# Attention's loads and stores wait, besides their product, for the landing that leaves at most 1.2 MB under way

## The chip, the cores and the metric

The kernel runs on one core of a Trainium2 chip. The metric is device microseconds (us) of one execution. Engines are named as the profile names them: PE (TensorE, matrix products), PEld (its weight loads), DVE (VectorE), ACT (ScalarE), POOL (GpSimd), SP (SyncE, which here only issues transfers).

## The reference

Attention over 8 batches, 8 heads, 576 positions and 64 dimensions, followed by a mixture of experts. In heads 0 to 3 a position sees the 32 positions up to itself, in heads 4 to 7 every fourth of the 128 positions up to itself:

```python
scores = scale * np.matmul(q, k.transpose(0, 1, 3, 2))
mask_plain = (rel >= 0) & (rel < window)                              # window 32
mask_dil = (rel >= 0) & (rel < window * dilation) & (rel % dilation == 0)   # dilation 4
scores = np.where(masks[None, :, :, :], scores, -1000000000.0)
attn = np.exp(scores - np.max(scores, axis=-1, keepdims=True))
attn = attn / (np.sum(attn, axis=-1, keepdims=True) + 1e-09)
out = np.matmul(attn, v)
```

The result, 4608 tokens of 512 numbers, goes through 8 experts. Each takes the 576 best tokens by `logits = x @ w_gate` (all pairs sorted, each token placed once) and computes `np.maximum(x @ w1[e], 0.0) @ w2[e]`.

## The kernel before

**Stages.** In the first 190 us or so the kernel computes attention and writes its rows into a scratch tensor `xd` in HBM, and prepares the choice of tokens. Behind it come eight rounds of expert products, which gather their tokens from `xd` and fetch weights. The change touches attention alone.

**Attention.** There are 32 units: per batch two kinds of heads (kind 0 plain, kind 1 dilated, in the names p and d) and two pairs of heads of each. For a batch and a kind SP issues two loads of q (`qs`, L376), two of k (L378) and two of v (L288). `qs` is then spread into `q` with zeros between (L389 on DVE and POOL, L284 on ACT; of kind 0 three of the four copies are POOL's, and the first pair of heads takes both of its halves from POOL). v is shifted into two other groups of partitions (L295, L297), from the second batch on by POOL alone. Per unit PE makes scores in bf16 for the row maxima (L492, L496), DVE reduces them, PE makes the scores in float32 (L503, L508), ACT takes the exponential (L462), PE multiplies with v (L515, L520), DVE divides (L528 to L530) into `xs`, and PE transposes the result (L579) for the gate's logits. Once a kind of a batch is done, SP stores `xs` into `xd` (L539): two transfers for kind 0, eight small ones for kind 1. q, k and v have two buffers for each kind, used in turn by the batches.

**What sets the order.** Attention is planned when the program is built: `Schedule.run` places every operation on its engine by estimated costs and due times, and each engine works its list off in order. SP's list is thus fixed: an instruction that waits holds up all loads and stores behind it. What a load or store of attention waits for is written by `paced` (L315). `K.gate` is the last product of a unit's scores, values or transposes that the plan has ended 0.2 us after the transfer's planned time at the latest; `after` makes the transfer wait for it. `LIMIT` is 1200e3 bytes and `flow` the list of earlier transfers. As long as the plan has no such product, the transfer waits for the landing of the earlier transfer with which it and all between them would be over 1.2 MB. In the kernel before this holds for the first ten loads (issued up to 7.6 us); every later one takes the `return` and waits for its product, and isn't entered into `flow`.

Besides this, each SP transfer uses one of eight completion semaphores in turn, and waits for the landing of the transfer eight places before it. The waits for buffers (q, k, v copied or used up, `xs` written) come on top.

Of the kernel before, what the change touches and what calls it, by code (L numbers as in the profile page):

```python
# [256 lines left out]
def attention(tc, ctx, C, load_const, T, xd, Lt, R):  # L257
# [5 lines left out]
    K = Schedule({"DVE": TOL_A, "ACT": TOL_B, "POOL": TOL_C, "PE": TOL_D}, True)  # L263
# [48 lines left out]
    def after(i, name, why):  # L312
        tc.add_manual_dep(i, name, mybir.DependencyInfo(mybir.DependencyClass.Sync, mybir.DependencyReason.DATA), reason=why)

    def paced(fn, bytes_):  # L315

        def run():
            i, under_way = fn().ins, bytes_
            if K.gate:
                return after(i, K.gate, "transfers keep step with the products")  # L320
            for prev, z in reversed(flow):
                under_way += z
                if under_way > LIMIT:
                    after(i, prev.name, "few bytes under way")
                    break
            flow.append((i, bytes_))

        return run
# [1182 lines left out]
```

## Time and profile before

| | us |
|---|---|
| median of 3 runs (684.36 to 690.0) | 687.72 |
| the profiled execution | 686.38 |
| its span, first to last instruction | 684.4 |

In the profile an instruction's row gives its start and length from the span's start, and in brackets the idle time of its engine before it and what ended that; "issue" means that the engine waited for nothing that the profile shows. A stretch A:B is given in us from the span's start. The landing of a transfer is when its last part is in place.

### The profile page before, as it was taken

What the parts mean: (1) busy time and instruction counts of PE and PEld (TensorE: products, weight loads), DVE (VectorE), ACT (ScalarE), POOL (GpSimd) and SP (SyncE); (2) the same over time, 40 slices, a digit from 0 to 9 for tenths busy, and PEclk for the clock granted to TensorE, in tenths of its full rate; (3) what the DMA queues carried; (4) which work ended last, traced back from release to release, by engine and by line L of the source; (5) the groups of instructions that cost most, each with busy time, mean ns of one, the idle gap of its engine ahead of it and who ended that gap; (6) DMA issues with size and microseconds to landing.
All of it is one profiled execution on the core that took longest, in us unless ns stands there. A gap on an engine that the chain in (4) does not pass through costs nothing.

```text
span 684.4 us, 18985 instructions
## 1 busy us (share of the span) xinstructions
PE 629.4 (92%) x7497; PEld 548.7 (80%) x7497; DVE 472.3 (69%) x1553; ACT 294.4 (43%) x643; POOL 207.8 (30%) x315
## 2 busy tenths in 40 slices
PE   7889887888955999999999999999999999999994
PEld 5778777677643998898799789889879989988983
DVE  6577856876668896689799689778969936714200
ACT  4646453455402835845345145234423625424210
POOL 5465576472003217433203112210320321311011
PEclk9999999999956999999999999999999999999998
DMA  8998988882203948977236115314512654203001
GB/s 245 267 273 241 211 250 243 229 225 67 73 1 116 246 78 211 259 163 235 83 95 229 47 55 184 133 55 139 177 47 66 228 201 146 69 32 102 1 26 44
DMA packets 51673, 99.09 MB, mean 145 GB/s; under 512 B 7168, under 2 KB 17152, under 8 KB 51584
## 3 DMA queue, kind: packets, MB, share of 16 engines
q1 hardware_dynamic: 42240, 72.71, 35.9%
q0 software_dynamic: 9344, 25.17, 13.6%
q8 instruction: 59, 0.97, 0.6%
q14 instruction: 30, 0.25, 0.1%
HBM read 72.69 MB, written 18.87 MB: 134 GB/s over the span
## 4 chain that ended last, share of the span: by engine, by line
PE 61%; issue 14%; DVE 14%; DMA 4%; POOL 3%; ACT 2%; SPq 0%; POOLq 0%; DVEq 0%; ACTq 0%
PE py L1378 18%; PE ph L1335 18%; PE px L520 4%; PE pS L508 4%; PE px L579 3%; PE ptx L1298 2%; PE pz L808 2%; PE py L1381 2%; PE py L1383 2%; DMA raw<-in_moe_w 1%; POOL out L1404 1%; DVE xs L530 1%; DVE hb L1356 1%; DVE mx L443 1%; DVE G L822 1%
## 5 line engine op out<-in xcount | busy, mean ns | idle before, releaser
L1378 PE MATMUL py<-w2h,hb 128*128 128x512 f32 x512 | 170.6, 399 | 0.0
L1335 PE MATMUL ph<-xh,w1h 128*128 128x256 f32 (+1 forms) x512 | 138.2, 300 | 0.0
L1335 PE MATMUL ph<-xl,w1h 128*128 128x256 f32 (+1 forms) x512 | 136.6, 297 | 0.0
L1335 PE MATMUL ph<-xh,w1l 128*128 128x256 f32 (+1 forms) x512 | 136.0, 296 | 0.0
L1378 PEld LDWEIGHTS py<-w2h,hb 128*128 128x128 f32 x512 | 96.1, 188 | 19.3
L1167 ACT ACTIVATE hb<-ph 128x256 fp32r<-128x256 f32 (+2 forms) x192 | 59.7, 345 | 95.3 <-PE ph L1335 93.9
L1404 POOL DMA_INDIRECT out<-y,idx x40 | 40.8, 1019 | 197.1 <-ACT y L1167 133.1
L1378 PE MATMUL py<-w2l,hb 128*128 128x512 f32 x256 | 99.8, 390 | 0.0
L1335 PEld LDWEIGHTS ph<-xh,w1h 128*128 128x128 f32 x512 | 91.8, 190 | 0.5
L1335 PEld LDWEIGHTS ph<-xh,w1l 128*128 128x128 f32 x512 | 91.7, 190 | 0.1
L1335 PEld LDWEIGHTS ph<-xl,w1h 128*128 128x128 f32 x512 | 91.4, 190 | 0.0
L1356 DVE SCALAR_TENSOR_TENSOR hb<-ph,hb 128x320 fp32r<-128x320 f32 (+1 forms) x128 | 56.6, 452 | 28.0 <-ACT hb L1167 25.1
L462 ACT ACTIVATE E<-pS 128x384 f32<-128x384 f32 x96 | 46.1, 489 | 56.9 <-PE pS L508 51.9
L1167 ACT ACTIVATE y<-py 128x512 f32<-128x512 f32 (+1 forms) x40 | 23.8, 596 | 92.4 <-PE py L1378 80.7
L508 PE MATMUL pS<-q,k 128*64 128x64 f32 x1152 | 54.8, 232 | 5.0 <-issue 5.0
L1284 POOL DMA_INDIRECT xg<-xd,idx x40 | 42.0, 1049 | 45.9 <-PE ph L1335 25.2
L520 PE MATMUL px<-v,E 128*64 128x65 f32 x1152 | 48.9, 226 | 6.7 <-issue 4.5
L1378 PEld LDWEIGHTS py<-w2l,hb 128*128 128x128 f32 x256 | 48.2, 188 | 8.5
L1167 ACT ACTIVATE w1h<-raw 128x512 fp32r<-128x512 f32 x64 | 40.1, 629 | 28.8 <-DMA raw<-in_moe_w 28.6
L520 PEld LDWEIGHTS px<-v,E 128*64 128x64 f32 x1152 | 43.3, 140 | 10.5 <-issue 6.7
L508 PEld LDWEIGHTS pS<-q,k 128*64 128x64 f32 x1152 | 46.0, 142 | 3.2 <-issue 3.2
L295 POOL COPY v<-v 32x520 f32<-32x520 f32 (+2 forms) x56 | 33.2, 618 | 50.2 <-DMA v<-in_vd 15.5
(193 smaller groups left out, 1110.0 us busy)
## 6 DMA issues: line engine op xcount, KB each, us to landing
raw<-in_moe_w SPq DMA_DIRECT2D x128, 256.0 KB, 3.5
qs<-in_qp SPq DMA_DIRECT2D x16, 288.0 KB, 7.0
k<-in_kp SPq DMA_DIRECT2D x16, 288.0 KB, 4.4
qs<-in_qd SPq DMA_DIRECT2D x16, 288.0 KB, 5.2
k<-in_kd SPq DMA_DIRECT2D x16, 288.0 KB, 6.8
xd<-xs SPq DMA_DIRECT2D x8, 512.0 KB, 4.9
w2l<-raw POOLq DMA_DIRECT2D x16, 256.0 KB
v<-in_vp SPq DMA_DIRECT2D x8, 325.0 KB, 7.0
```

The costliest lines, as they stand in the source:

```text
L295: f(t[:32, c0 + 1:c1 + 1], t[96:, c0:c1])
L462: e = self.op("ACT", 490, lambda j=j, pS=pS: nc.scalar.activation(self.E[:, 3 * j:3 * j + 3].rearrange("p c x -> p (c x)"), pS.tile[:, :38 ...
L508: x = nc.tensor.matmul(pS[64 * h:64 * h + 64, k, :, h], self.K[:, 32 * g:32 * g + 64], self.Q[:, g], start=False, stop=True, skip_group_ch ...
L520: x = nc.tensor.matmul(px[64 * h:64 * h + 64, c - c0, a], self.E[:, k, 64 * a:64 * a + 64], self.V[:, k, 2 * self.ui + a], start=True, sto ...
L579: x = nc.tensor.transpose(pt.tile[:, 128 * (c - c0):128 * (c - c0) + 128], xs[:, c, 2 * ui:2 * ui + 2].rearrange("p a d -> p (a d)"), C["i ...
L808: nc.tensor.matmul(o, self.ohr[:, j].rearrange("p r x -> p (r x)"), self.G[:, 4 * j:4 * j + 4, :w], start=(j == 0), stop=(j == NCH // 4 - 1))
L1167: act = lambda o, i, f=AF.Copy: nc.scalar.activation(o, i, f)
L1284: nc.gpsimd.indirect_dma_start(out=xg[:n], out_offset=None, in_=xd, in_offset=bass.IndirectOffsetOnAxis(ap=box[0][:n, m:m + 1], axis=0))
L1335: nc.tensor.matmul(o, a[:, d * 128:d * 128 + 128], b[:, d, c0:c1], start=((d, i) == pairs[0]), stop=((d, i) == pairs[-1]))
L1356: hl = op("DVE", 335 if j == 0 else 400, lambda: nc.vector.scalar_tensor_tensor(hb[:, CAP + c0:CAP + c1], o, 0.0, hb[:, c0:c1], op0=OP.max ...
L1378: nc.tensor.matmul(py, x, w, start=(f + i == 0), stop=(f == NF - 1 and i == 2))
L1404: s = nc.gpsimd.indirect_dma_start(out=out, out_offset=bass.IndirectOffsetOnAxis(ap=box[0][:n, m:m + 1], axis=0), in_=y[:n], in_offset=None)
```

## The change

One `return` goes. A transfer that waits for its product now also goes through the rule of 1.2 MB and is entered into `flow`.

```diff
         def run():
             i, under_way = fn().ins, bytes_
             if K.gate:
-                return after(i, K.gate, "transfers keep step with the products")
+                after(i, K.gate, "transfers keep step with the products")
             for prev, z in reversed(flow):
                 under_way += z
                 if under_way > LIMIT:
                     after(i, prev.name, "few bytes under way")
                     break
             flow.append((i, bytes_))
```

No instruction moves: all engines have the same rows in the same order. On SP the waits of 121 of the 450 rows differ. `DMAHW0` to `DMAHW7` are the eight completion semaphores of SP's transfers, `PE`, `DVE`, `Activation` and `Pool` those of the engines; a wait that an earlier one on SP already implies is not written. Here is SP's list in the third batch, before:

```order
L378 DMA k00_95<-in_kp 128x576 [waits DMAHW5_49,PE_49]
L288 DMA v00_103<-in_vp 64x1300 [waits DMAHW6_49,PE_49,Activation_49]
L288 DMA v00_103<-in_vp 64x1040 [waits DMAHW7_49,PE_49,Activation_49]
L539 DMA xd_66<-xs01_124 128x4x256 [waits DMAHW0_49,DVE_49,PE_49]
L539 DMA xd_66<-xs01_124 64x256 [waits DMAHW1_49,PE_49]
L376 DMA qs10_109<-in_qd 128x576 [waits DMAHW2_49,PE_49,Activation_49]
L376 DMA qs10_109<-in_qd 128x576 [waits DMAHW3_49,PE_49]
L378 DMA k10_97<-in_kd 128x576 [waits DMAHW4_49,PE_49]
```

And the same eight rows of the changed kernel:

```order
L378 DMA k00_95<-in_kp 128x576 [waits DMAHW5_49,DMAHW0_49,PE_49]
L288 DMA v00_103<-in_vp 64x1300 [waits DMAHW3_49,DMAHW6_49,PE_49,Activation_49]
L288 DMA v00_103<-in_vp 64x1040 [waits DMAHW7_49,PE_49,Activation_49]
L539 DMA xd_66<-xs01_124 128x4x256 [waits DMAHW5_49,DVE_49,PE_49]
L539 DMA xd_66<-xs01_124 64x256 [waits DMAHW1_49,PE_49]
L376 DMA qs10_109<-in_qd 128x576 [waits DMAHW2_49,DMAHW6_49,PE_49,Activation_49]
L376 DMA qs10_109<-in_qd 128x576 [waits DMAHW7_49,PE_49]
L378 DMA k10_97<-in_kd 128x576 [waits DMAHW4_49,DMAHW0_49,PE_49]
```

The store of 128x4x256 now waits for `DMAHW5`, the landing of the k load three rows above it, and the last k load for `DMAHW0`, the landing of that store, four rows above it; before, both waited for a transfer eight places back.

The second place is SP's list in the fifth batch, the last loads of kind d and the first of the next batch. Before:

```order
L378 DMA k10_97<-in_kd 128x576 [waits DMAHW6_49,PE_49]
L539 DMA xd_66<-xs01_124 128x4x256 [waits DMAHW7_49,DVE_49,PE_49]
L539 DMA xd_66<-xs01_124 64x256 [waits DMAHW0_49,PE_49]
L378 DMA k10_97<-in_kd 128x576 [waits DMAHW1_49]
L288 DMA v10_105<-in_vd 64x1300 [waits DMAHW2_49,PE_49,Pool_49]
L288 DMA v10_105<-in_vd 64x1040 [waits DMAHW3_49,PE_49,Pool_49]
L376 DMA qs01_108<-in_qp 128x576 [waits DMAHW4_49,PE_49,Pool_49]
```

And in the changed kernel:

```order
L378 DMA k10_97<-in_kd 128x576 [waits DMAHW6_49,DMAHW2_49,PE_49]
L539 DMA xd_66<-xs01_124 128x4x256 [waits DMAHW4_49,DMAHW7_49,DVE_49,PE_49]
L539 DMA xd_66<-xs01_124 64x256 [waits PE_49]
L378 DMA k10_97<-in_kd 128x576 [waits DMAHW5_49]
L288 DMA v10_105<-in_vd 64x1300 [waits DMAHW7_49,PE_49,Pool_49]
L288 DMA v10_105<-in_vd 64x1040 [waits DMAHW3_49,PE_49,Pool_49]
L376 DMA qs01_108<-in_qp 128x576 [waits DMAHW0_49,PE_49,Pool_49]
```

The first v load of kind d now waits for `DMAHW7`, the landing of the large store three rows above it, where before it waited for `DMAHW2`, a load eight places back.

## Rows read from the trace of the kernel before

**Rows 1.** Busy time by stretch: us, then busy us (and instructions) of PE, PEld, DVE, ACT, POOL, then the granted clock of PE (1.00 is 2.4 GHz), the mean busy share of the 16 DMA engines, and the GB/s that they moved.
```profile
41.00:154.70 113.70, 95.75 (x2618) 84.70 (x2616) 80.54 (x256) 57.32 (x124) 68.33 (x109) 0.98 0.89 240
3.60:11.60 8.00, 5.93 (x102) 4.83 (x101) 4.80 (x11) 3.11 (x5) 7.16 (x17) 1.00 0.97 255
...
154.70:222.00 67.30, 48.41 (x965) 36.82 (x958) 47.54 (x186) 20.69 (x47) 10.64 (x15) 0.80 0.20 60
```

**Rows 2.** PE's instructions in order of time, those in attention before which PE stood with "issue": start, length, line, operation, tiles, and in brackets the idle time.
```profile
48.51 0.46 PE L520 MATMUL px<-v,E 128*64 128x65 f32 x9 [1.12 <-issue]
70.70 0.40 PE L520 MATMUL px<-v,E 128*64 128x65 f32 x7 [1.68 <-issue]
91.66 0.51 PE L508 MATMUL pS<-q,k 128*64 128x64 f32 x11 [1.89 <-issue]
98.99 0.22 PE L503 MATMUL pS<-R,const 73*64 73x64 bf16 x3 [0.85 <-issue]
104.09 0.22 PE L508 MATMUL pS<-q,k 128*64 128x64 f32 x1 [1.00 <-issue]
109.73 0.28 PE L503 MATMUL pS<-R,const 73*64 73x64 bf16 x6 [1.97 <-issue]
115.66 0.22 PE L503 MATMUL pS<-R,const 73*64 73x64 bf16 x2 [0.79 <-issue]
120.23 0.22 PE L508 MATMUL pS<-q,k 128*64 128x64 f32 x1 [0.87 <-issue]
146.69 0.27 PE L520 MATMUL px<-v,E 128*64 128x65 f32 x1 [1.44 <-issue]
156.26 0.46 PE L508 MATMUL pS<-q,k 128*64 128x64 f32 x9 [1.21 <-issue]
```

**Rows 3.** DMA queues: packets, MB, share of 16 engines. The first row is of the whole span, the second of the stretch 89:90.2.
```profile
q8 instruction: 59, 0.97, 0.6%
...
q8 instruction: 1, 0.02, 5.3%
```

**Rows 4.** SP's transfers in order of time from 82 to 92 us: start, length, line, tiles, count.
```profile
82.12 1.86 SPq L376 DMA_DIRECT2D qs<-in_qd  x2
84.08 0.38 SPq L378 DMA_DIRECT2D k<-in_kd  x1
84.56 0.94 SPq L539 DMA_DIRECT2D xd<-xs  x2
85.56 1.11 SPq L378 DMA_DIRECT2D k<-in_kd  x1
86.77 1.26 SPq L288 DMA_DIRECT2D v<-in_vd  x2
88.26 1.90 SPq L376 DMA_DIRECT2D qs<-in_qp  x2
```

**Rows 5.** From issue to landing, of single loads, in this order, of 288 KB each: the q loads issued at 11.28, 26.93, 82.12 and 88.26 us, the k load issued at 38.54 us, and (325 KB) the v load of kind d issued at 66.38 us.
```profile
DMA to landing us min/median/max: 5.2/5.2/5.2
DMA to landing us min/median/max: 4.5/4.5/4.5
DMA to landing us min/median/max: 5.7/5.7/5.7
DMA to landing us min/median/max: 8.8/8.8/8.8
DMA to landing us min/median/max: 5.3/5.3/5.3
DMA to landing us min/median/max: 9.9/9.9/9.9
```

**Rows 6.** Issues of the whole span: tiles, operation, count, KB of one, median us from issue to landing where it is known.
```profile
qs<-in_qp SPq DMA_DIRECT2D x16, 288.0 KB, 7.0
...
xd<-xs SPq DMA_DIRECT2D x8, 512.0 KB, 4.9
...
v<-in_vp SPq DMA_DIRECT2D x8, 325.0 KB, 7.0
```

**Rows 7.** SP's transfers in order of time in the third batch, as in Rows 4.
```profile
38.54 1.47 SPq L378 DMA_DIRECT2D k<-in_kp  x2
40.12 2.00 SPq L288 DMA_DIRECT2D v<-in_vp  x2
42.23 1.47 SPq L539 DMA_DIRECT2D xd<-xs  x2
```

**Rows 8.** POOL's and PE's instructions in order of time: POOL's first copy of a v of kind d behind its idle time (with what ended that), its copies of q behind it, and the first product of PE that needs these.
```profile
76.43 0.83 POOL L295 COPY v<-v 32x780 f32<-32x780 f32 x1 [4.95 <-PE pm L496]
...
81.55 2.08 POOL L389 COPY q<-qs 64x576 f32<-64x576 f32 x3
82.96 0.35 PE L496 MATMUL pm<-k,q 128*64 128x64 bf16 x10
95.39 0.83 POOL L295 COPY v<-v 32x780 f32<-32x780 f32 x1 [3.77 <-PE px L579]
...
104.25 0.33 PE L496 MATMUL pm<-k,q 128*64 128x64 bf16 x8
137.00 1.00 POOL L295 COPY v<-v 32x780 f32<-32x780 f32 x1 [5.30 <-DMA v<-in_vd]
...
147.43 0.35 PE L496 MATMUL pm<-k,q 128*64 128x64 bf16 x10
```

## The prediction

> **What bounds the kernel now.** The change lies in attention's loads, so I read the time by stretches first, then what stands idle inside attention, and only then the transfers. From 41 us, where all loads are paced by products, to 154.7 us, where the last load lands, PE is busy for 95.75 of 113.7 us and the DMA engines have a busy share of 0.89 [rows 1]. Two resources are thus near their limit together. Behind the last load the DMA share is 0.20 [rows 1], so nothing there hangs on the pacing; what attention gains or loses passes to the end undiminished.
>
> PE's 17.95 idle us in that stretch have one main owner. Ten times PE stands for 0.8 to 2.0 us with nothing in the profile that it waits for; the nine before 154.7 us are 1.12 + 1.68 + 1.89 + 0.85 + 1.00 + 1.97 + 0.79 + 0.87 + 1.44 = 11.6 us, and with the one at 156.26 it is 12.8 us [rows 2]. What is missing is the instructions. The instruction queue moved 59 packets of 0.97 MB in all, and one of them fell into 89 to 90.2 us [rows 3], right before PE resumes at 91.66 [rows 2]; it went through the same DMA engines as the loads. The transfers issued between 84.08 and 88.26 us, two k, the store of 512 + 64 KB, both v and one q, are 2025 KB or 2.07 MB [rows 4, 6], and the last of them took 8.8 us to land [rows 5]. No stall of this kind stands before 47 us, where loads landed within 4.5 to 5.3 us [rows 2, 5]. So I read these stalls as PE running dry because its next packet came late behind a deep queue. The trace doesn't show when a packet was asked for, so this step is an inference.
>
> [...]
>
> **What the change does, part by part.**
>
> *Removed: nothing that is executed.* No instruction goes or moves; SP's own extra waits cost it a few hundredths of a us each and are hidden, since SP spends most of this stretch waiting anyway. I count them at nothing.
>
> *Added: on 121 rows of SP's list another landing to wait for, closer than the eighth transfer back.* Four loads of 288 KB fit into 1.2 MB (1.18 MB); with a v of 325 KB in the set only three transfers do (901 KB, 0.92 MB); the store of 512 KB leaves room for the two v loads ahead of it and no more (1097 KB, 1.12 MB) [rows 6]. At the first place in the order the store behind 42.23 us waits for the second k issued behind 38.54 us. The first of these two took 5.3 us [rows 5, 7], so the second lands at about 45 us and the store is some 3 us late; queued behind it on SP are both q and both k of kind d, and the k then wait for the store itself. At the second place the v of kind d, issued at 86.77 [rows 4], waits for the store of 84.56.
>
> *Gained: PE's stalls.* With at most 1.2 MB ahead of an instruction packet I expect nearly all 12.8 us of them to go, if the loads keep up. At least nothing of it, if the depth isn't the cause.
>
> *Lost: the rate of the loads.* The trace has no stretch of attention with this rule throughout, so I bound the rate from both sides. Upper end: from 3.6 to 11.6 us most loads ran under this very rule, and the DMA moved 255 GB/s at a share of 0.97 [rows 1], more than the 240 of the later stretch. Lower end: bytes under way divided by the time to landing. About 1.1 MB are under way on average, and a load that was issued into a queue of about this depth took 4.5, 5.2, 5.3 or 5.7 us [rows 5]. At 5.6 us that is 196 GB/s, at 4.5 us 244. I take 5.0 us, the mean of the first three, and 220 GB/s: each wait closes a loop of landing, issue and start, in which the last of 16 engines counts. The bytes from 41 to 154.7 us are 113.7 us x 240 GB/s = 27.3 MB. At 220 GB/s they need 124.1 us, so the stream slips by 10.4 us over this stretch; at 255 GB/s 107.1 us (6.6 us ahead), at 196 GB/s 139.3 us (25.6 us late).
>
> *What of a late load reaches PE.* The tightest path runs through POOL: it stands idle until a v of kind d lands (66.38 + 9.9 = 76.3 us, and POOL starts at 76.43 [rows 5, 8]), shifts it, then copies q, and PE's next unit starts 6.5 us behind POOL's start, at 82.96: no slack. The next such place has 104.25 - 95.39 - 6.5 = 2.4 us of slack, the one at 147.43 has 147.43 - 137.00 - 6.5 = 3.9 us [rows 8]. With a slip in proportion to time (10.4 us x (t - 41) / 113.7) the landings are late by 3.2 us at 76.4, 5.0 at 95.4 and 8.8 at 137. Now the two go together, place by place:
> - 82.96: PE is 3.2 us late; the stalls that went before it (1.12 + 1.68) are eaten by this wait.
> - 104.25: 3.2 less the stalls between (1.89 + 0.85 + 1.00 = 3.7) is -0.5; the load asks for 5.0 - 2.4 = 2.6. The later one decides: +2.6.
> - 147.43: 2.6 less 5.1 (1.97 + 0.79 + 0.87 + 1.44) is -2.5; the load asks for 8.8 - 3.9 = 4.9. It decides: +4.9.
> - End of attention: 4.9 less the stall at 156.26 (1.21) is +3.7.
>
> **The sum.** The profiled execution took 686.38 us; 686.4 + 3.7 = 690.1, say 690 us. That is 0.3% above the median of the runs shown, 687.72, and a measurement of this kernel tells about 1%: no change that can be told, with the stalls gone and waits for loads in their place. What is late next is v of kind d on POOL.
>
> **The rivals.**
>
> *The stream keeps up (faster).* The rate stays at 255 GB/s, as from 3.6 to 11.6 us, and gates move ahead with PE. For it: a DMA share of 0.97 under this rule [rows 1]. Against it: that stretch has no stores. The stream could be 6.6 x 0.84 = 5.6 us ahead at 137 us, so -5.6 - 3.9 - 1.2 = -10.7 us, short of the full 12.8: 675.7 us.
>
> *The stream falls behind (slower).* SP stands at a landing, then at a product, in order, while the queue drains; the store of 512 KB ties up nearly the whole allowance. It decides from the point at which the landing at 137 us is over 12 us late (12 - 3.9 - 1.2 = 6.9 us, 1%), that is a slip of 14.3 us in the stretch, 213 GB/s or 5.2 us to a landing at 1.1 MB. For it: that is close to what I take, and a 5.7 [rows 5] is among the rows. Against it: shallower queues may shorten landings. At 5.45 us, 202 GB/s: 135.1 us, 21.4 late, 18.1 at 137, +13.0: 699.4 us.
>
> *Depth isn't the cause of the stalls.* The packet is late for its own reason and the stalls stay. Then PE has only the waits: 3.2, 2.6, 4.9, the largest of them +4.9: 691.3 us. For it: the trace doesn't show the asking. Against it: the long stalls stand where the queue was deepest. [...]
>
> **How the numbers follow.** Forecast 0.36, stream keeps up 0.22, stream falls behind 0.34, depth not the cause 0.08. The forecast and the last rival lie within 1%, so: faster by over 1% 0.22, within 1% 0.44, slower by over 1% 0.34. The range takes in the faster case and the slower one's value and leaves the ends (full 12.8 us gained and more; 196 GB/s) out: 676 to 701 us. The forecast's own range is 682 to 694.6.
>
> **What would show it.** Right: PE's waits with "issue" between 41 and 160 us fall from 12.8 us to under 4; landings of loads fall to 4 to 5.5 us; SP's waits for landings grow; POOL's idle time before v of kind d grows; GB/s from 41 us on falls to about 220 and the last load lands near 165 us. The step on the rate is wrong if the GB/s stay at 240 or above, the step on the stalls if "issue" stays near 12.8 us, and the step on the path if PE's place of 82.96 us moves without POOL's.

## The result: 1.3% slower

| | before | after |
|---|---|---|
| median, us | 685.68 (6 runs, 683.04 to 690.0) | 694.93 (6 runs, 691.8 to 698.7) |
| ratio to before | | 1.0126, 95% interval 1.0089 to 1.0163 |
| the profiled execution, us | 686.38 | 698.7 |
| its attention ends at, us | 187.71 | 195.05 |

The forecast was 690 us and no change that can be told. The time lies inside the range of 676 to 701, 0.3 us outside the forecast's own range of 682 to 694.6, and the kernel is slower by 6.1 to 11.2 us. The attention of the profiled execution is 7.34 us longer. That end is ACT's last copy for the gate's logits, first before, then after:

```profile
187.71 0.17 ACT L284 ACTIVATE Lt<-px 64x8 f32<-64x8 f32 x1 [2.30 <-DVE Lt L693]
```

```profile
195.05 0.17 ACT L284 ACTIVATE Lt<-px 64x8 f32<-64x8 f32 x1 [2.30 <-DVE Lt L693]
```

The profiled execution is the slowest of its six: it lost another 5 us among the experts, where ACT and DVE stood with no cause that the trace names. Of the 13 other profiled executions below one (spread15) has the same wait of ACT, 5.4 us, and twelve have none, most of the kernels with the rule among them. Nothing below rests on it, and attention's 7.3 us lie inside the interval by themselves:

```profile
336.05 0.60 ACT L1167 ACTIVATE xh<-ptx 128x512 fp32r<-128x512 f32 x1 [5.46 <-remote]
```

**The profile after.** Busy time by stretch, columns as in [rows 1], whose first two stretches come first; the clock is a share of the full one, and no row shows it in GHz:

```profile
41.00:154.70 113.70, 91.83 (x2424) 81.69 (x2424) 73.45 (x239) 53.54 (x117) 64.70 (x103) 0.95 0.79 223
3.60:11.60 8.00, 5.98 (x102) 4.84 (x101) 4.95 (x11) 3.80 (x6) 7.61 (x17) 1.00 0.98 278
...
20.00:24.00 4.00, 2.58 (x39) 2.27 (x41) 1.07 (x3) 2.48 (x5) 1.11 (x2) 0.82 0.88 297
24.00:28.00 4.00, 4.00 (x114) 4.00 (x112) 1.84 (x7) 3.02 (x7) 1.08 (x3) 0.75 0.71 176
84.00:88.00 4.00, 2.71 (x86) 2.47 (x88) 2.00 (x7) 1.38 (x4) 3.55 (x6) 1.00 0.24 63
104.00:108.00 4.00, 2.90 (x88) 2.52 (x85) 2.99 (x10) 1.66 (x3) 3.89 (x7) 1.00 0.48 142
...
112.00:116.00 4.00, 4.00 (x108) 4.00 (x106) 1.40 (x5) 0.98 (x2) 1.42 (x2) 0.66 0.99 249
...
144.00:148.00 4.00, 4.00 (x29) 3.90 (x27) 0.36 (x2) 3.25 (x8) 0.44 (x1) 0.50 0.92 229
```

In the long stretch the DMA engines are less busy: 0.79 and 223 GB/s where [rows 1] has 0.89 and 240. The loss isn't even: from 84 to 88 us they moved 63 GB/s, from 104 to 108 us 142. In the kernel before, the lowest stretch at the corresponding stores (issued from 92.73 us on) is

```profile
96.00:100.00 4.00, 3.15 (x99) 2.87 (x99) 2.32 (x8) 0.97 (x4) 3.88 (x8) 1.00 0.40 110
```

PE's waits from 41 to 175 us (what it waited for, us in total, times, longest), the counterpart of [rows 2]:

```profile
PE pm L496 <- DMA k<-in_kp: 5.4, 2, 3.8
PE px L579 <- DVE xs L530: 2.8, 1, 2.8
PE px L520 <- POOL q L389: 1.7, 1, 1.7
...
PE pm L496 <- DMA k<-in_kd: 1.2, 2, 0.9
PE pm L496 <- POOL q L389: 1.2, 1, 1.2
PE px L520 <- POOL v L297: 0.9, 1, 0.9
PE pS L503 <- issue: 0.6, 1, 0.6
PE pS L508 <- issue: 0.2, 1, 0.2
```

"Issue" is down to 0.8 us. In its place stand loads: k directly (6.6 us), q and v by way of POOL (3.8), and q of kind d by way of DVE (2.8). The last is a path that one finds only by following two engines: DVE copies q in the middle of its list, stands there for the load, and PE waits for the `xs` behind it.

```profile
139.18 1.31 DVE L389 COPY q<-qs 64x576 f32<-64x576 f32 x2 [2.69 <-DMA qs<-in_qd]
...
141.41 0.77 PE L579 MATMUL px<-const,xs 128*128 128x128 f32 x5 [2.80 <-DVE xs L530]
```

SP's transfers in order of time, as in [rows 4, 7]:

```profile
81.65 5.28 SPq L539 DMA_DIRECT2D xd<-xs  x8
87.03 0.37 SPq L378 DMA_DIRECT2D k<-in_kp  x1
...
98.04 1.11 SPq L288 DMA_DIRECT2D v<-in_vd  x2
...
102.27 5.28 SPq L539 DMA_DIRECT2D xd<-xs  x8
107.64 1.53 SPq L378 DMA_DIRECT2D k<-in_kp  x2
```

The eight small stores of kind 1 hold SP for 5.28 us each time, for 576 KB in all, and the k loads come behind them; these are the stretches in which the DMA engines moved little. SP's waits for landings have grown from 7.9 us in the kernel before to 49.6 us, both from 41 to 155 us. The five largest in the changed kernel:

```profile
SPq L288 <- DMA qs<-in_qp: 7.2, 3, 3.3
SPq L378 <- DMA v<-in_vp: 6.2, 4, 2.2
SPq L378 <- DMA v<-in_vd: 5.5, 4, 2.0
SPq L539 <- DMA v<-in_vd: 4.8, 4, 1.9
...
SPq L539 <- DMA v<-in_vp: 3.7, 1, 3.7
```

And the places of [rows 8], POOL's and PE's instructions in order of time:

```profile
80.50 0.83 POOL L295 COPY v<-v 32x780 f32<-32x780 f32 x1 [5.67 <-PE pm L448]
...
85.63 2.08 POOL L389 COPY q<-qs 64x576 f32<-64x576 f32 x3
87.05 0.35 PE L496 MATMUL pm<-k,q 128*64 128x64 bf16 x10 [1.20 <-POOL q L389]
...
102.26 0.83 POOL L295 COPY v<-v 32x780 f32<-32x780 f32 x1 [4.78 <-PE pm L496]
...
111.07 0.35 PE L496 MATMUL pm<-k,q 128*64 128x64 bf16 x10 [3.77 <-DMA k<-in_kp]
...
147.56 0.83 POOL L295 COPY v<-v 32x780 f32<-32x780 f32 x1 [4.45 <-DMA v<-in_vd]
...
154.88 0.35 PE L496 MATMUL pm<-k,q 128*64 128x64 bf16 x10
```

At the first place PE starts 6.55 us behind POOL, as before, and now the trace names POOL's q as the cause. At the second it is k itself: issued at 107.64, used at 111.07, where before it was issued at 98.79.

### The profile page after: what moved, and what is told of

Its sections match the earlier page's. It is cut to its first block, busy times and chain, and to the rows that moved or that the text cites. A ratio compares the mean times of both kernels' runs of the same rounds, so it can differ in the third digit from the quotient of the medians.

```text
span 696.9 us, 18979 instructions
## 1 busy us (share of the span) xinstructions
PE 634.5 (91%) x7497; PEld 553.9 (79%) x7497; DVE 472.1 (68%) x1553; ACT 295.2 (42%) x643; POOL 207.0 (30%) x315
## 4 chain that ended last, share of the span: by engine, by line
PE 50%; DVE 17%; issue 13%; DMA 11%; POOL 3%; ACT 2%; SPq 1%; another core or an unknown queue 0%; POOLq 0%; DVEq 0%; ACTq 0%
PE py L1378 16%; PE ph L1335 15%; PE px L520 3%; DMA raw<-in_moe_w 2%; PE px L579 2%; DMA v<-in_vp 2%; PE ptx L1298 2%; PE pS L508 2%; DVE hb L1356 2%; DMA qs<-in_qd 1%; DVE G L822 1%; PE pz L808 1%; PE py L1381 1%; PE py L1383 1%; DMA qs<-in_qp 1%
## 5 line engine op out<-in xcount | busy, mean ns | idle before, releaser
L508 PE MATMUL pS<-q,k 128*64 128x64 f32 x1152 | 55.3, 234 | 0.2 <-issue 0.2
L1284 POOL DMA_INDIRECT xg<-xd,idx x40 | 40.4, 1010 | 45.7 <-PE ph L1335 25.4
L508 PEld LDWEIGHTS pS<-q,k 128*64 128x64 f32 x1152 | 46.6, 144 | 0.0
```

The source lines that it names most:

```text
L508: x = nc.tensor.matmul(pS[64 * h:64 * h + 64, k, :, h], self.K[:, 32 * g:32 * g + 64], self.Q[:, g], start=False, stop=True, skip_group_ch ...
L1284: nc.gpsimd.indirect_dma_start(out=xg[:n], out_offset=None, in_=xd, in_offset=bass.IndirectOffsetOnAxis(ap=box[0][:n, m:m + 1], axis=0))
```

## The experiments

Two questions were open. Are PE's stalls a matter of the depth? And where does the loss come from: from every landing wait alike ("every wait costs"), from the store of 512 KB, which takes up nearly half of the allowance ("the big store"), or from the fact that 1.2 MB don't last while SP issues little ("reserve")? All runs in one table. The ratio is to the kernel before; the end of attention, PE's "issue" and its direct waits for loads (both from 41 to 175 us) and the GB/s from 41 to 154.7 us are of the one profiled execution.

| kernel | limit, MB | median | ratio, 95% interval | attention ends | issue | loads | GB/s |
|---|---|---|---|---|---|---|---|
| before | none | 685.68 | 1 | 187.71 | 13.3 | 0 | 240 |
| lim18 | 1.8 | 687.54 | 0.9962 (0.9926 to 0.9997) | 186.18 | 10.1 | 0 | 242 |
| lim15 | 1.5 | 681.96 | 0.9945 (0.9915 to 0.9976) | 183.00 | 2.5 | 0.3 | 244 |
| after | 1.2 | 694.93 | 1.0126 (1.0089 to 1.0163) | 195.05 | 0.8 | 6.6 | 223 |
| lim09 | 0.9 | 725.16 | 1.0529 (1.0450 to 1.0608) | 223.31 | 1.7 | 7.9 | 186 |
| third | 1.2 from 38.5 us on | 690.80 | 1.0074 (1.0047 to 1.0101) | 192.35 | 2.6 | 6.6 | 228 |
| bigfree | 1.2, not the big store | 692.66 | 1.0064 (1.0029 to 1.0099) | 192.80 | 4.5 | 5.5 | 230 |
| two_before | none | 682.92 | 0.9913 (0.9882 to 0.9944) | 183.44 | 6.8 | 0 | 241 |
| two_after | 1.2 | 687.08 | 0.9971 (0.9936 to 1.0007) | 188.67 | 2.4 | 1.3 | 236 |
| spread_before | none | 687.76 | 0.9989 (0.9959 to 1.0020) | 192.50 | 16.6 | 0.8 | 232 |
| spread_after | 1.2 | 691.32 | 1.0021 (0.9991 to 1.0052) | 192.15 | 5.3 | 1.0 | 232 |
| spread15 | 1.5 | 684.41 | 0.9918 (0.9888 to 0.9949) | 182.67 | 7.1 | 0 | 245 |
| spread18 | 1.8 | 683.54 | 0.9953 (0.9925 to 0.9981) | 185.15 | 9.4 | 0.7 | 242 |
| early | none | 693.93 | 1.0062 (1.0020 to 1.0104) | 191.26 | 11.2 | 3.0 | 238 |

The last four columns scatter from one execution to the next: attention of the profiled spread_before ends 4.8 us later than that of the kernel before, while the ratio is 0.9989.

Medians of different sets of runs aren't to be compared (the kernel before had 685.7 to 690.4 in them); the ratios are, and where one stands in the text its interval is in the table.

**The size of the allowance.** One number changes (1800e3, 1500e3, 900e3).

```diff
-LIMIT, PACE, B_D = 1200e3, 300.0, 6000
+LIMIT, PACE, B_D = 1800e3, 300.0, 6000
```

lim18, expected:

> The changed kernel with its limit at 1.8 MB in place of 1.2. Theory 'reserve': a queue of 1.2 MB holds 4.9 us of work at 245 GB/s, and SP needs 5.3 us for the eight small stores of kind 1, so the queue runs dry behind each group of them (63 GB/s from 84 to 88 us) and k is late; 1.8 MB hold 7.3 us, so PE's direct waits for k (6.6 us in the changed kernel) fall under 2 us and the last load of v lands before 160 us (168.3 with 1.2 MB). If PE's stalls without a cause come from the depth, some come back, 3 to 7 us of the 12.8. Sum 680 to 687 us, ratio to before 0.992 to 1.002. Rival 'every wait costs': the loss is spread over all landing waits and shrinks with their number only: 688 to 692 us, the last load after 162 us. Rival 'depth isn't the cause of the stalls': the stalls are all back (over 10 us) at 1.8 MB or none is, with no relation to the depth.

lim15, expected:

> The changed kernel with its limit at 1.5 MB and the small stores in a row as they were. 'Reserve': 1.5 MB last 6.1 us at 245 GB/s, barely more than the 5.3 us of the eight stores: PE's waits for k between those with 1.2 MB (6.6 us) and with 1.8 MB (none), 2 to 4 us, stalls without a cause 3 to 7 us, 685 to 690 us, ratio 0.994 to 1.002, behind the same limit with the stores spread (0.992).

lim09, expected:

> The changed kernel with its limit at 0.9 MB. Theory 'reserve' and the prediction's step on the rate: three loads of 288 KB under way, about 0.8 MB on average at 4.0 us to a landing, are 200 GB/s where 1.2 MB gave 223; 27.3 MB then take 136 us in place of 122, so the last v of kind d lands 12 to 18 us later still (180 to 186 us) and the time is 704 to 714 us. Stalls without a cause stay under 1.5 us. A rival by which the loss has little to do with the size of the allowance gives 694 to 699 us.

With 1.8 MB the loads are on time (no direct wait of PE for them) and most stalls are back, 10.1 us in place of the 3 to 7 expected. "Over 10 us" was named as the sign that the depth is not their cause; the series further below decides against that, not this run. PE's waits with "issue" in that kernel, columns as above:

```profile
PE pm L496 <- issue: 3.2, 2, 2.5
PE px L520 <- issue: 2.6, 4, 1.2
PE pS L503 <- issue: 2.3, 2, 2.0
PE pS L508 <- issue: 2.0, 3, 1.0
```

With 1.5 MB both are small: 2.5 us of stalls, 0.3 for loads, attention 4.7 us shorter than before. That is better than expected (3 to 7 us, 2 to 4 us, 685 to 690 us). The stretch 41 to 154.7 us and one with the eight small stores in it (SP's row below) show why; columns as in [rows 1] and [rows 4]:

```profile
41.00:154.70 113.70, 99.49 (x2755) 87.30 (x2755) 84.73 (x268) 59.56 (x129) 70.69 (x112) 1.00 0.87 244
...
92.00:96.00 4.00, 4.00 (x76) 3.41 (x75) 0.50 (x3) 3.06 (x10) 0.00 (x0) 1.00 0.98 220
96.00:100.00 4.00, 3.64 (x131) 3.53 (x128) 2.94 (x9) 2.13 (x4) 3.85 (x7) 1.00 0.64 198
```

```profile
92.52 7.10 SPq L539 DMA_DIRECT2D xd<-xs  x8
99.71 0.85 SPq L378 DMA_DIRECT2D k<-in_kp  x2
```

SP is with the small stores for 7.10 us, and the DMA engines still move 220 and 198 GB/s. With 0.9 MB the loss is far larger than expected (725.16 where 704 to 714 was said): 186 GB/s, and attention ends 35.6 us later. From 0.9 to 1.2 to 1.5 MB the stream gains 37 and then 21 GB/s, from 1.5 to 1.8 nothing. So 1.2 MB lie below the knee of this series, and the rule as such, at 1.5 MB, is worth 0.2 to 0.9%.

**Fewer small stores.** Kind 1's rows in two stores of the same bytes, with the rule and without. The rows go to other places of `xd`, so these two kernels don't compute the reference's result.

```diff
-                for f, rows in stores(b, kind, xs):
+                for (f, rows), z in zip(stores(b, kind, xs), (256, 224, 192, 160, 128, 96, 64, 32) if kind else (1024, 128)):
-                    usex.append(op("SP", 475, paced(f, rows * 512), ...))
+                    usex.append(op("SP", 475, paced(f, rows * 512) if f else (lambda: None), ...))
...
-            row = (DIL if kind else 1) * DM
+            row = DM
...
+        put(0, 4, 0, 128, 0, 128)
+        put(4, 1, 0, 64, 512, 1)
+        if kind:
+            out += [(None, 0)] * 6
...
```

two_after, expected:

> The changed kernel, but the rows of kind 1 are stored by two transfers of 512 and 64 KB, as those of kind 0 are, in place of eight small ones of the same bytes in all; they go to other rows of the scratch tensor, so its contents differ. All other lists stay in order. SP is then busy for 1.5 in place of 5.3 us with these stores. 'Reserve': the queue no longer runs dry, no stretch of 4 us between 41 and 155 us moves under 110 GB/s because of them, PE's waits for k fall from 6.6 us to under 2, and the time is within 3 us of the kernel before with the same two stores (the changed kernel stands 9 us above the kernel before). 'Every wait costs': the distance to the kernel before with two stores stays 7 to 11 us. 'The big store ties up the allowance': there are twice as many big stores, so the distance grows to 11 us and more.

two_before, expected:

> The kernel before with the same two stores for kind 1 (rows stored at other places of the scratch tensor, bytes the same): the reference for the changed kernel with two stores. All theories: SP has some 3.8 us less to issue per batch, which matters little beside a queue of 2 MB, 682 to 688 us. As the eighth transfer back is now further back in bytes, the queue can be deeper: by the reading that PE's stalls without a cause come from the depth they stay at 10 us or grow.

Both ran in one set, so the distance between them can be taken: 687.08 - 682.92 = 4.2 us, where the change alone had 8.6 (1.26% of 685.7): about half. By the scatter of the ten runs of each, 2 to 6 us are possible. "Reserve" said under 3, "every wait costs" 7 to 11, "the big store" over 11: the last two don't hold, and the small stores are part of the loss, about half, not all. The gap from 84 to 88 us is gone (250 GB/s with the rule and two stores), and PE waits 1.3 us for k. The stalls are 6.8 us without the rule, where 10 or more were expected from a deeper queue, and 2.4 with it.

**The big store out of the rule.** It waits for its product alone and isn't counted.

```diff
-            if K.gate:
-                after(i, K.gate, "transfers keep step with the products")
+            if K.gate and after(i, K.gate, "transfers keep step with the products") is None and bytes_ > 400e3:
+                return
```

> The changed kernel with the store of 512 KB neither waiting for the rule of 1.2 MB nor counted in it (it waits for its product alone). 'The big store ties up the allowance': most of the loss goes, 683 to 688 us, and the last load of v lands before 161 us. 'Reserve': the small stores still empty the queue, the gain is under 4 us, 690 to 695 us, and the stretches under 110 GB/s behind the small stores stay. 'Every wait costs': 1 to 3 us of gain, 692 to 694 us.

1.0064 in place of 1.0126, some 4 us: at the upper edge of what "reserve" allowed, and far from "most of the loss". The time, 692.66, is also inside what "every wait costs" allowed (692 to 694); the run doesn't tell these two apart. The low stretches stay, columns as in [rows 1]:

```profile
84.00:88.00 4.00, 3.41 (x118) 3.17 (x115) 2.93 (x11) 1.46 (x3) 2.85 (x5) 1.00 0.34 84
104.00:108.00 4.00, 2.01 (x59) 1.78 (x56) 2.25 (x9) 1.12 (x3) 3.65 (x6) 1.00 0.28 74
```

So both count: what uses up the allowance and what keeps SP from issuing. By the medians, to take either away gives back about half of the loss. Both together were not run, and with the big store free up to 0.5 MB more is under way, so part of this gain may be that of a higher limit.

**The small stores spread.** Planned as before, but issued two behind each of the next four loads (batches 0 to 4).

```diff
-    first, flow = [1e8], []
+    first, flow, later = [1e8], [], []
...
-    def sp(cost, fn, deps, bytes_, b, kind=0):
+    def sp(cost, fn, deps, bytes_, b, kind=0, go=lambda run: (run(), [later.pop(0)() for _ in later[:2]])):
...
-        return op("SP", 475 * cost, paced(fn, bytes_) if cost == 1 else fn, deps,
+        return op("SP", 475 * cost, (lambda run=paced(fn, bytes_): go(run)) if cost == 1 else fn, deps,
...
-op("SP", 475, paced(f, rows * 512), Unit.xsd, ...)
+op("SP", 475, (lambda f=f, rows=rows: later.append(paced(f, rows * 512))) if kind and b < B - 3 else paced(f, rows * 512), Unit.xsd, ...)
```

spread_after (1.2 MB), expected:

> The changed kernel (1.2 MB) with the eight small stores of kind 1 moved on SP's list, two of them behind each of the next four loads, for batches 0 to 4; everything else stays in order. Theory 'reserve' (the queue of 1.2 MB is emptied where SP issues little for long: at the eight small stores in a row, and where the store of 512 KB takes up the allowance): the part that belongs to the small stores goes, as it did with two stores in their place: PE's waits for k fall from 6.6 to under 2.5 us, the last v of kind d lands 4 to 6 us earlier (162 to 164 us), 688 to 691 us, ratio 1.000 to 1.004. PE's stalls without a cause stay under 3 us. Rival 'every wait costs': the number of waits is the same, so 693 to 696 us.

spread15, expected:

> The same spread of the small stores, with the limit at 1.5 MB. 1.5 MB let the two v loads and the store of 512 KB (1.12 MB) be joined by another load of 288 KB. 'Reserve' with stalls that come from the depth: 3 to 6 us of stalls in place of 12.8, the last v lands at 155 to 159 us, 681 to 686 us, ratio 0.988 to 0.997. 'Every wait costs': 689 to 692 us.

spread_before, expected:

> The kernel before (no rule of 1.2 MB behind 7.6 us) with the small stores of kind 1 spread in the same way, two behind each of four loads. It tells whether the gain of the kernel with 1.5 MB and spread stores (ratio 0.992) is the spread's alone. 'Reserve': a queue of 2 MB hides the eight stores in a row anyway, so the spread alone brings under 2 us: 687 to 691 us, ratio 0.997 to 1.003, stalls without a cause at 9 to 14 us. If the spread is all of it: 682 to 686 us.

spread18, expected:

> Small stores spread, limit at 1.8 MB. If the stalls follow the depth they are 7 to 10 us, as with 1.8 MB and the stores in a row, and nothing more is to be won on the loads: 685 to 689 us, behind 1.5 MB with the stores spread. If the depth didn't matter any more, it would be as fast as that one, 682 to 685 us.

With 1.2 MB the waits for k fall from 6.6 to 1.0 us and the ratio from 1.0126 to 1.0021: against "every wait costs", since the number of waits is the same. Stalls came back though (5.3 us; under 3 was expected). Without the rule the spread brings nothing (0.9989) and the stalls grow to 16.6 us, more than the 9 to 14 expected. With 1.5 MB it is 0.9918, which its interval doesn't tell from 1.5 MB with the stores in a row. Both beat the kernel before and the changed one. With 1.8 MB the stalls are 9.4 us, as expected if they follow the depth; the time, 683.54, lies where the other reading had it, and 0.9953 isn't told from 1.5 MB either.

**The rule from the third batch on.** The first 29 transfers that have a product stay out of it.

```diff
-    first, flow = [1e8], []
+    first, flow, n = [1e8], [], []
...
-            if K.gate:
-                after(i, K.gate, "transfers keep step with the products")
+            if K.gate and (after(i, K.gate, "transfers keep step with the products"), n.append(i), len(n) < 30)[2]:
+                return
```

> The changed kernel, but the rule of 1.2 MB begins only with the second k of the third batch (38.5 us), where the prediction let the slip begin; the earlier transfers stay out of it as in the kernel before. The prediction's step put no slip before 41 us; in the changed kernel PE's wait for the constants at 21 us is 1.7 us longer. If that early slip is carried to the end, attention ends 1.5 us earlier than in the changed kernel (5.8 in place of 7.3 us behind the kernel before), 691 to 694 us; if later slack takes it up, attention ends 7 us behind the kernel before as in the changed kernel.

Attention ends at 192.35, 2.7 us earlier than in the changed kernel where 1.5 was expected, and the ratio is 1.0074. That was to show an early slip carried to the end, and in the times it looks so; PE's rows show it otherwise. PE's product at 21.2 us starts at the same time in both kernels, but in the changed one PE had stood for 2.72 us before it, and what follows runs at a granted clock of 0.50 (22.60 to 25.90 us; 1.00 in the kernel before). First before, then after (in the kernel before twelve products of L508, at 22.74 us, take 0.57 us):

```profile
21.21 1.09 PE L579 MATMUL px<-const,xs 128*128 128x128 f32 x8 [1.00 <-DMA const<-in_cf]
```

```profile
21.30 1.09 PE L579 MATMUL px<-const,xs 128*128 128x128 f32 x8 [2.72 <-DMA const<-in_cf]
...
22.82 0.93 PE L508 MATMUL pS<-q,k 128*64 128x64 f32 x12
```

The granted clock was 0.82 and 0.75 in the two stretches of 4 us from 20 us (above); with the rule from the third batch on it was 1.00 in both, and no time was lost there. But PE made this up soon: its product of 48.51 us [rows 2], before which it had stood, starts at 48.71 in the changed kernel. At 137.84 us the changed kernel is level again with the one of this run. Here is the row of this run first, then that of the changed kernel:

```profile
137.95 0.77 PE L579 MATMUL px<-const,xs 128*128 128x128 f32 x5
```

```profile
137.84 0.77 PE L579 MATMUL px<-const,xs 128*128 128x128 f32 x5
```

The next row of PE makes the difference: 2.80 us of waiting for `xs` behind q of kind d in the changed kernel (141.41 above), 0.38 in this one. The load of that q was issued at 133.33 there and at 129.65 here. It is thus the stream of loads that stayed behind, not PE, and both ends are of one execution each.

**A deeper queue.** The kernel before, with each transfer waiting for an earlier product.

```diff
-                self.gate = next((m for e, m in reversed(self.marks) if e <= t + 200), None)
+                self.gate = next((m for e, m in reversed(self.marks) if e <= t - 3000), None)
```

> The kernel before, without the rule of 1.2 MB, with every transfer of attention waiting for a product that the plan ends 3.2 us earlier than the one it waits for now: the same lists, a deeper queue. If PE's stalls without a cause come from the depth, they grow from 12.8 to 15 to 22 us while loads land earlier: 687 to 694 us. If the depth is not their cause, they stay at 11 to 14 us and the time is 682 to 687 us.

The stalls, 11.2 us, are what was said for the case that the depth is not their cause; the time, 1.0062, is what was said for the other. Each transfer still waits for the eighth before it, and the queue did not get deeper (0.77 MB under way on average where the kernel before has 0.76, estimated as below); PE waited 3.0 us for loads. So this run decides nothing on the depth.

**What follows on the stalls.** In each of the three series they grow with the limit: 0.8, 2.5, 10.1, 13.3 us (1.2, 1.5, 1.8 MB, none); with the spread 5.3, 7.1, 9.4, 16.6; with two stores 2.4 and 6.8. Only 0.9 MB (1.7) falls out of order. These are single executions, but the order is the same three times.

The traces also hold every packet of the instruction queue with its start and length. In the 14 profiled executions PE stood 67 times for over 0.5 us with "issue" (41 to 175 us). 62 of these waits end 1.1 to 1.8 us after such a packet has ended; of its 116 equally long waits for other engines or loads 14% do. The longest wait with "issue" in spread_before, and the instruction queue from 148.8 to 150.1 us, columns as in [rows 2, 3]:

```profile
151.30 0.22 PE L520 MATMUL px<-v,E 128*64 128x65 f32 x1 [3.16 <-issue]
```

```profile
q8 instruction: 1, 0.02, 5.4%
```

So 62 of 67 waits end close behind a packet, as the prediction's inference wants it. That PE had stood for what the packet held remains the author's reading: no row shows whose instructions a packet holds. The other five waits (1.4 to 1.7 us) all stand before one and the same product of the third batch, and the one of 0.9 MB is among them; what they waited for is open. The packets themselves took 1.0 to 1.2 us in the median of every kernel (1.16 us in the kernel before and 1.07 in the changed one, from 41 to 154.7 us). Whether they are asked for late or stand behind the loads, no row shows; the view counts their time in the share of the same 16 engines (1.3% of it in the kernel before, from 41 to 155 us) and doesn't say which engine moved one.

How deep the queue was can be estimated from the traces, as what SP had issued less what its queue had moved, on average from 41 to 154.7 us: 0.76 MB before, 0.69 in spread_before, 0.68 with 1.8 MB, 0.62 in spread15, 0.61 in spread18 and with 1.5 MB, 0.59 in two_before, 0.49 with 1.2 MB and 0.36 with 0.9. In the 2 us before the start of a packet behind which such a wait ended it was 0.77 MB, before the others 0.48. Two_before was thus shallower than the kernel before, not deeper as expected, and its fewer stalls fit. The mean alone doesn't settle the stalls: 0.61 to 0.62 MB go with 2.5, 7.1 and 9.4 us.

## Where the prediction was right, and why its sum fell short

*The stalls* (expected under 4 us): 0.8. Such waits ended close behind an instruction packet in 62 of 67 cases and shrink with the limit in three series, so the rival that they stay whatever the depth falls; that a deep queue makes a packet late was the author's inference, and no row shows it. Part of the fall is no cure: with 1.2 MB and few waits for loads (spread) 5.3 us are left, 3.7 without the one of unknown cause, so some were only covered by the waits.

*The rate* (taken 220 GB/s from bounds of 196 and 255): 223. The upper bound, 255 from a stretch without stores [rows 1], was of no use for one with them; that stretch, in which both kernels have the same rule, moved 278 in the profiled execution of the changed kernel. Times from SP's issue to the engine that stood for the load are 107.64 to 111.07 and 87.03 to 90.6, 3.4 and 3.6 us for k, 143.02 to 147.56, 4.5 us for v; nothing like the 9.9 us of [rows 5] is among them. At 223 GB/s these times mean 0.8 to 1.0 MB under way, where the forecast divided 1.1 MB by 5.0 us: both were too large, and that 220 came so close is in part luck. The last v of kind d reaches POOL 12.9 us later (166.83 for 153.92), where the slip was put at 10.4.

*What of it reaches PE* is the step that failed in size:

| | predicted | measured |
|---|---|---|
| POOL's start at 76.43 | +3.2 | 80.50, +4.1 |
| PE's unit at 82.96 | +3.2 | 87.05, +4.1 |
| POOL's start at 95.39 | +5.0 | 102.26, +6.9 |
| PE's unit at 104.25 | +2.6 | 111.07, +6.8 |
| POOL's start at 137.00 | +8.8 | 147.56, +10.6 |
| PE's unit at 147.43 | +4.9 | 154.88, +7.5 |
| end of attention | +3.7 | +7.3 |

- The slip was counted from 41 us, though most transfers from 11 us on came under the rule too. POOL's places are 0.9, 1.9 and 1.8 us later than said. With the rule from the third batch on, attention ended 2.7 us earlier, by way of the loads.
- The path was taken to be v alone. At 104.25 v by way of POOL asks for 102.26 + 6.5 = 108.8, 4.5 us late; k, queued behind eight small stores that themselves wait for v's landing, came at 111.07. The prediction had named SP's order for the 512 KB store and not for these eight.
- At 147.43 the landing would give 10.6 - 3.9 = 6.7, but v didn't hold PE there: its row at 154.88 shows no wait, PE came 7.5 us late by itself. It was 3.0 us late before the wait behind q of kind d, and 8.95 after it:

```profile
134.83 1.53 PE L579 MATMUL px<-const,xs 128*128 128x128 f32 x10
139.61 0.34 PE L496 MATMUL pm<-k,q 128*64 128x64 bf16 x9
```

```profile
148.56 0.49 PE L496 MATMUL pm<-k,q 128*64 128x64 bf16 x9
```

  The first two rows are the kernel before; their places in the changed kernel are 137.84 (above) and 148.56. Of the 5.9 us between, 2.8 are the wait, and most of the rest fell into a stretch in which PE ran at a granted clock of 0.50 (144 to 148 us, above). The sum had neither the load of q of kind d nor the clock. What the clock alone cost was not tested.
- The stall at 156.26 (1.2 us) was counted as a gain at the end. Only 7.45 - 7.34 = 0.1 came of it: a stall of 0.6 us and other waits took its place.

In the prediction's own terms +3.7 becomes about +7.3 by 1.8 (v's later landing), 0.8 and 1.1. That is bookkeeping and not the path: what came last went through q of kind d and the stretch at a clock of 0.50. The k at 104.25 cost the middle of attention. Its +6.8 shrank to 3.0 by 137.84 us, and the stalls that were gone between make up 1.97 + 0.79 + 0.87 = 3.6 us of it [rows 2]; from 112 to 116 us both kernels have a lowered clock, 0.74 before and 0.66 after.

*SP's own waits* (put at a few hundredths of a us each): its 97 wait instructions from 41 to 155 us of the changed kernel took 0.028 us in the median.

*What was said of the set under way*, that with a v of 325 KB in it only three transfers fit, holds beside loads of 288 KB alone; both v loads (325 and 260 KB) and two of 288 KB are 1161 KB, 1.19 MB, and fit. The sum doesn't use it.

*The rivals.* "The stream falls behind" (699.4) was to decide from 213 GB/s and a landing 12 us late at 137 us; it was 223 and 10.6, so it didn't hold by its own condition, though its words (SP stands in order while the queue drains) say what the low stretches show, and its outcome, slower by over 1%, is what the median gives (1.3%, interval from 0.9). The measured time lies between the forecast and this rival, and inside the range because the range was made to take in the rival's value. The stream's rate of 255 didn't come.

## What to carry to other kernels

A first estimate for a limit on bytes under way is the longest time in which the issuing engine adds little, times the rate (here 5.3 us of small stores at 240 GB/s, 1.3 MB). Above it, at 1.5 MB, both costs were small here; below it, at 1.2 and 0.9, the gaps were not made up again (223 and 186 GB/s). It is rough: with 1.5 MB SP was with these stores for 7.10 us, 1.7 MB by the same product, and the stream held. Between 1.2 and 1.5 MB the sign of the change turned, so such a limit wants two or three values tried, not one argued. Follow a late load through every engine that waits for it in its own order: here k went straight to PE, v by POOL and q by DVE.

## What the runs showed of the hardware that was not expected

- Behind its three waits of over 2.5 us from 20 to 175 us PE worked in the changed kernel at a granted clock below 1.00 for some us: behind 2.72 us at 21.3 (0.82 and 0.75), behind 3.77 us at 111.07 (0.66), behind 2.80 us at 141.41 (0.50 from 144 to 148). Twelve products of L508 took 0.93 us behind the first of these waits (22.82 us), 0.57 in the kernel before (22.74 us). It isn't so behind every wait: behind 2.48 us at 88.83 with 1.8 MB, and behind 2.96 us at 107.38 with 0.9 MB, eleven or twelve of them took 0.54 to 0.57 us, up to the rows of 90.24 and 110.19 us. In the kernel with 1.5 MB the stretch from 41 to 154.7 us has 1.00.
- Limit on the bytes under way and rate from 41 to 154.7 us: 186 GB/s at 0.9 MB, 223 at 1.2, 244 at 1.5, 242 at 1.8, 240 with eight transfers and no limit.
- PE stood 16.6 us of attention with "issue" in one execution of a kernel with 0.8 us of direct waits for loads (spread_before), and all but 1.7 us of its longer stalls ended 1.1 to 1.8 us behind an instruction packet.
